# Low parts of the attention output and the gate: from VectorE subtracts to TensorE and ScalarE

## The chip, the cores and the metric

The kernel runs on one core of one Trainium2 chip. The metric is the device time of one execution in microseconds (us), the median of three runs. A NeuronCore has five engines, each with its own in-order queue of instructions: TensorE (PE in the profile; PEld is its weight load), VectorE (DVE), ScalarE (ACT), GpSimd (POOL) and SyncE (SP, which here only issues transfers). They work side by side and wait for one another through semaphores. SBUF is the on-chip memory; PSUM is the memory that TensorE accumulates into, eight banks of 512 float32 columns in 128 partitions.

## The reference

Three stages follow one another; batch 8, sequence 576, eight heads of 64, model width 512, hidden width 2048. The middle one is where the change lies.

```python
# 1: attention inside chunks of 64 tokens
scores = scale * np.matmul(q_c, k_c.transpose(0, 1, 2, 4, 3))
scores = scores - np.max(scores, axis=-1, keepdims=True)
attn = np.exp(scores)
attn = attn / (np.sum(attn, axis=-1, keepdims=True) + 1e-09)
out = np.matmul(attn, v_c)
# 2: x = out with the heads side by side; causal convolution of 5 taps per feature, gate
gate = 1.0 / (1.0 + np.exp(-gate_pre))
val = x @ w_val
y = gate * val @ w_out
# 3: normalised rows, two-layer network, residual
xn = (y - mu) / np.sqrt(var + 1e-06) * g_ln
out = y + np.maximum(xn @ w_ch1, 0.0) @ w_ch2
```

All of it is float32. The large products use a faster float32 form of TensorE that rounds its operands (`fp32r`), and so the kernel splits an operand in a high part (the rounded copy) and a low part (what the rounding took off) and adds three products: high by high, low by high, high by low.

## The kernel before

The 4608 tokens are cut in 18 units of 256 tokens and 9 blocks of 512 (two units each), numbered 0 to 8. A loop of slots, one per unit, carries several stages of different units side by side:

- `a3(u)`: scores of unit u on TensorE (32 small matmuls into `sc`), then the softmax: VectorE takes the maximum (`mx`), subtracts it (`ex`), ScalarE takes the exponential, VectorE sums (`sm`), inverts and multiplies (`pr`).
- `a4(u-1)`: TensorE transposes the probabilities into PSUM (`pst`), ScalarE copies them out (`pT`).
- `a5(u-1)`: TensorE multiplies with v (32 small matmuls into the PSUM tile `x`, features by tokens). ScalarE copies `x` twice: to `xf` (float32, with a halo of four tokens, for the convolution; L233) and to `xh` (the high part; L236). VectorE writes the low part `xl` = `x` - `xh` (L238). Where a sequence ends inside the unit, all of these are cut in two. The tiles `x` and `pst` share one buffer of two PSUM banks.
- `conv(j, f)` for block j and feature tile f (four tiles of 128): one scaled copy on ScalarE (L248) and four steps on VectorE into `cg` (L250), so 16 VectorE steps a block. `sigm(j)`: one sigmoid over the whole of `cg` on ScalarE (L257).
- `val(j, f)`: a chain of 12 matmuls of 512 columns into one PSUM bank (`psv`). VectorE multiplies it with the gate into `gv` in SBUF (L290, in two pieces where a sequence ends inside the block), ScalarE copies `gv` to the high part `gh` (L293), VectorE writes the low part `gl` = `gv` - `gh` (L294).
- `proj(j, t)`: four chains of 12 matmuls (`pso`) from `gh`, `gl` and the output weights; ScalarE copies the result to `y` and sends it to memory.

Between these, VectorE, ScalarE and GpSimd decode and split weights (lines 87 to 96: `da`, and the tiles that are made from it).

The order in which each engine meets its instructions is fixed when the program is built. For the first four slots TensorE's order is as written; after that a list scheduler places all instructions by its own estimate of when they become ready, and pieces under `tc.high_priority()` go first. Within a block of the steady stretch TensorE's order is: value chains 0 and 1, scores, value chain 2, transposes, value chain 3, `x`, projection chains 0 and 1, scores, projection chain 2, transposes, projection chain 3, `x`. After the attention (331 us into the span) comes the two-layer network, which the change does not touch.

Of the kernel before, what the change touches and what calls it, by code (L numbers as in the profile page):

```python
# [8 lines left out]
F32 = mybir.dt.float32  # L9
F32R = mybir.dt.float32r  # L10
U32 = mybir.dt.uint32
ACTF = mybir.ActivationFunctionType
ALU = mybir.AluOpType
# [6 lines left out]
def tile_chunk_attention_gated_mlp(ctx: ExitStack, tc: tile.TileContext, qk, v, w_val, conv_w, w_out, g_ln, w1, w2, out):  # L20
    nc = tc.nc
# [9 lines left out]
    P = 128  # L31
    BLK = 512
    UN = 256
    UPB = BLK // UN
    NB = NT // BLK
    NU = NT // UN
    NP = H // 2
# [3 lines left out]
    LAG = 1  # L41
# [28 lines left out]

    ident = const.tile([P, P], F32, name="ident")
    cw = const.tile([P, (KC + 1) * CT], F32, name="cw")
    gr = const.tile([CT, P], F32, name="gr")


# [112 lines left out]
            nc.scalar.activation(out=t, in_=ps, func=ACTF.Copy)  # L188
            pT[u] = t

    xf, xh, xl = {}, {}, {}

    def new_block(j):
        o = boundary(j)
# [13 lines left out]
    def a5(u):  # L208
# [4 lines left out]
        for i in range(NP // 2):  # L213
            for c in range(NC):
                n, cs = c // 2, slice(c % 2 * CH, (c % 2 + 1) * CH)
                for f in range(2):
                    for r in range(2):
                        r0, o0 = CH * r, CH * f
                        nc.tensor.matmul(
                            out=x[o0:o0 + CH, r, i, c * CH:(c + 1) * CH],  # L220
                            lhsT=va[r0:r0 + CH, c, 2 * i + f, :],
                            rhs=t[r0:r0 + CH, n * NP + 2 * i + f, cs],
                            start=True, stop=True,
                        )
        if uu == 0:
            new_block(j)
# [3 lines left out]
        with tc.high_priority():  # L230
            for lo, hi, sh in segs:
                dst = xf[j][:, :, lo + sh:hi + sh].rearrange("p (r i) t -> p r i t", r=2)
                nc.scalar.activation(out=dst, in_=x[:, :, :, lo - a:hi - a], func=ACTF.Copy)  # L233
            for lo, hi, sh in segs:
                dst = xh[j][:, :, lo:hi].rearrange("p (r i) t -> p r i t", r=2)
                nc.scalar.activation(out=dst, in_=x[:, :, :, lo - a:hi - a], func=ACTF.Copy)  # L236
                low = xl[j][:, :, lo:hi].rearrange("p (r i) t -> p r i t", r=2)
                nc.vector.tensor_tensor(out=low, in0=x[:, :, :, lo - a:hi - a], in1=dst, op=ALU.subtract)  # L238


    cg = pD1.tile([P, CT, BLK + HALO], F32, name="cg")

# [31 lines left out]
    def val(j, f):  # L274
# [8 lines left out]
            ops += [(hs[c][:, fs], xh[j][:, c, :]), (hs[c][:, fs], xl[j][:, c, :]), (ls[c][:, fs], xh[j][:, c, :])]  # L283
        chain(ps, ops)
        o = boundary(j)
        gv = pD2.tile([P, BLK], F32, tag="gv", name="gv")
        with tc.high_priority():
            for lo, hi, sh in ((0, o, 0), (o, BLK, HALO)):
                if lo < hi:
                    nc.vector.tensor_tensor(out=gv[:, lo:hi], in0=ps[:, lo:hi], in1=cg[:, f, lo + sh:hi + sh], op=ALU.mult)  # L290
            a = pD1.tile([P, BLK], F32R, tag=f"gh{f}", name="gh")
            b = pD1.tile([P, BLK], F32R, tag=f"gl{f}", name="gl")
            nc.scalar.activation(out=a, in_=gv, func=ACTF.Copy)  # L293
            nc.vector.tensor_tensor(out=b, in0=gv, in1=a, op=ALU.subtract)  # L294
        gh[j, f], gl[j, f] = a, b

    def proj(j, t):
        hs, ls = wv["os"]
# [285 lines left out]


    make_identity(nc, ident)
    load_qkv(0)
    load_w(w_val, "v", 0)
    load_qkv(1)
# [12 lines left out]
    def slot(u):  # L602
# [14 lines left out]
        if LAG <= u < NU + LAG:  # L617
            a5(u - LAG)
        warm(u, 3)
        for fn in d[2] + d[3]:  # L620
            fn()

    dense = {}
# [1 line left out]
    def at(u, i, fn):  # L625
        dense.setdefault((u, i), []).append(fn)
# [42 lines left out]
    for j in range(NB):  # L669
# [11 lines left out]
            at(u + 1, 2, lambda j=j: sigm(j))  # L681
        for f in range(CT):
            at(*[(u + 1, 2), (u + 1, 3), (u + 2, 0), (u + 2, 1)][f], lambda j=j, f=f: val(j, f))
        for t in range(BLK // P):
            at(*[(u + 2, 2), (u + 2, 3), (u + 3, 0), (u + 3, 1)][t], lambda j=j, t=t: proj(j, t))
    for f in range(NFA):
# [122 lines left out]
```

## Time and profile before

| | |
|---|---|
| median of three runs | 1122.77 us (1122.62 to 1123.02) |
| the profiled execution | 1124.26 us, its span 1122.4 us |
| busy: PE, PEld | 1069.3 us (95%), 866.7 us (77%) |
| busy: DVE, ACT, POOL | 715.7 us (64%), 482.0 us (43%), 108.8 us (10%) |

The span is what the profiler saw of the program; the rest of the execution's time lies around it. A share of busy time is a mean over stages with different limits. TensorE's matmuls are pipelined, so their durations overlap and the distance from one start to the next tells what one costs. In a timeline, "[idle before <-releaser]" is the time for which the engine stood before the instruction, and what ended it.

### The profile page before, as it was taken

Reading aid. Unit: us, or ns where it says so; the run is one execution under the profiler, and the core shown is the slowest. Engines: PE = TensorE matmul, PEld = TensorE weight load, DVE = VectorE, ACT = ScalarE, POOL = GpSimd, SP = SyncE. Lnnn points to the kernel's source line nnn. Section 1 sums busy time; section 2 is a strip of 40 time slices with the busy share of each in tenths; the row PEclk is TensorE's granted clock in tenths of the full one; section 3 lists DMA queues with packets and bytes.
Section 4 is the critical chain, followed back from the end, with each engine's and each line's share of the span. In section 5 each row is a group of like instructions: output and inputs, shape, how many; then the busy total and the mean of one; then the engine's idle time right before and its main releaser. Section 6 shows DMA issues by size and latency. Waiting matters only on the chain.

```text
span 1122.4 us, 17077 instructions
## 1 busy us (share of the span) xinstructions
PE 1069.3 (95%) x6862; PEld 866.7 (77%) x6862; DVE 715.7 (64%) x1171; ACT 482.0 (43%) x832; POOL 108.8 (10%) x120
## 2 busy tenths in 40 slices
PE   5798999999998988899999999999999999999998
PEld 5676777777786866688888788888888888878877
DVE  6999999999949877446557434457443547432434
ACT  3576666766666654344433233333233333121221
POOL 2021100000004434222210000000000000000000
PEclk9898999999999999999999999999999999999999
DMA  8544554551245635343344533233533223622212
GB/s 338 171 142 160 172 177 142 198 181 47 71 165 187 209 112 211 137 150 131 115 149 131 194 107 113 94 113 124 195 113 113 85 94 108 211 94 94 75 38 75
DMA packets 58581, 155.28 MB, mean 138 GB/s; under 512 B 5742, under 2 KB 13958, under 8 KB 56198
## 3 DMA queue, kind: packets, MB, share of 16 engines
q1 hardware_dynamic: 53318, 144.75, 37.8%
q10 hardware_dynamic: 5184, 9.44, 2.3%
q8 instruction: 54, 0.88, 0.3%
q14 instruction: 25, 0.20, 0.1%
HBM read 116.41 MB, written 37.75 MB: 137 GB/s over the span
## 4 chain that ended last, share of the span: by engine, by line
PE 62%; DVE 27%; issue 4%; ACT 4%; DMA 2%; POOL 0%; SPq 0%; POOLq 0%; ACTq 0%; DVEq 0%
PE acc L507 15%; PE x L533 15%; PE psf L507 15%; PE zy L533 10%; DVE cg L250 8%; DVE da L90 2%; DVE da L89 2%; DVE mx L167 2%; DVE sm L176 2%; DVE xl L238 1%; PE acc L393 1%; DVE gv L290 1%; DVE pr L179 1%; DVE gl L294 1%; PE pso L264 1%
## 5 line engine op out<-in xcount | busy, mean ns | idle before, releaser
L553 DVE TENSOR_TENSOR c<-x,c 128x512 f32<-128x512 f32 x96 | 66.2, 690 | 237.6 <-ACT c L549 181.6
L507 PE MATMUL acc<-w,h 128*128 128x512 f32 x768 | 186.8, 392 | 0.0
L507 PE MATMUL psf<-w,h 128*128 128x512 f32 x768 | 186.0, 391 | 0.0
L507 PEld LDWEIGHTS acc<-w,h 128*128 128x128 f32 x768 | 144.9, 189 | 31.7
L507 PEld LDWEIGHTS psf<-w,h 128*128 128x128 f32 x768 | 144.2, 188 | 31.3
L533 PE MATMUL x<-t,wc 128*128 128x512 f32 x576 | 146.9, 390 | 3.4 <-DVE c L553 3.4
L549 ACT ACTIVATE c<-zy 128x512 f32<-128x512 f32 x96 | 57.9, 604 | 188.8 <-PE zy L533 188.7
L533 PEld LDWEIGHTS x<-t,wc 128*128 128x128 f32 x576 | 108.0, 188 | 27.3 <-DVE c L553 4.3
L544 ACT ACTIVATE h<-c 128x512 fp32r<-128x512 f32 x96 | 60.5, 630 | 136.7 <-DVE c L553 136.1
L250 DVE SCALAR_TENSOR_TENSOR cg<-xf,cw,cg 128x516 f32<-128x516 f32 (+1 forms) x176 | 109.1, 660 | 0.1
L512 DVE TENSOR_TENSOR yt<-psf,yt 128x512 f32<-128x512 f32 x128 | 88.1, 690 | 25.1 <-PE psf L507 21.1
L533 PE MATMUL zy<-b,wc 128*128 128x512 f32 x384 | 98.9, 393 | 0.0
L533 PEld LDWEIGHTS zy<-b,wc 128*128 128x128 f32 x384 | 71.2, 188 | 14.6
L545 DVE SCALAR_TENSOR_TENSOR h<-c,h 128x512 fp32r<-128x512 f32 x96 | 68.4, 713 | 14.1 <-ACT h L544 13.9
L264 PE MATMUL pso<-oh,gh 128*128 128x512 f32 x144 | 60.8, 423 | 5.6 <-ACT gh L293 5.4
L264 PE MATMUL pso<-oh,gl 128*128 128x512 f32 x144 | 57.7, 411 | 6.7 <-DVE gl L294 6.7
L96 POOL TENSOR_TENSOR w<-da,w 128x512 fp32r<-128x512 f32 x32 | 47.5, 1489 | 136.6 <-ACT w L95 135.3
L264 PE MATMUL psv<-xh,vh 128*128 128x512 f32 x144 | 59.1, 411 | 0.0
L264 PE MATMUL pso<-ol,gh 128*128 128x512 f32 x144 | 57.9, 402 | 0.0
L264 PE MATMUL psv<-xl,vh 128*128 128x512 f32 x144 | 56.7, 393 | 0.0
L264 PE MATMUL psv<-xh,vl 128*128 128x512 f32 x144 | 56.6, 393 | 0.0
L533 PE MATMUL x<-b,wc 128*128 128x512 f32 x192 | 52.2, 408 | 4.4 <-DVE h L545 3.7
(108 smaller groups left out, 1556.6 us busy)
## 6 DMA issues: line engine op xcount, KB each, us to landing
wc<-wc SPq DMA_DIRECT2D x112, 512.0 KB, 3.3
qkr<-in_qk SPq DMA_DIRECT2D x18, 1024.0 KB, 6.1
raw<-in_moe_w_ch SPq DMA_DIRECT2D x32, 512.0 KB, 4.1
vr<-in_v SPq DMA_DIRECT2D x18, 512.0 KB, 4.4
yd<-y ACTq DMA_DIRECT2D x36, 256.0 KB, 2.6
out<-yt SPq DMA_DIRECT2D x36, 256.0 KB, 3.7
yr<-yd SPq DMA_DIRECT2D x32, 256.0 KB, 3.4
yt<-yd SPq DMA_DIRECT2D x32, 256.0 KB, 4.1
```

What stands on the lines that cost most here:

```text
L89: nc.vector.scalar_tensor_tensor(out=au, in0=hw, scalar=0x80000000, in1=au, op0=ALU.bitwise_and, op1=ALU.bitwise_or)
L90: nc.vector.scalar_tensor_tensor(out=au, in0=lw, scalar=29, in1=au, op0=ALU.logical_shift_right, op1=ALU.bitwise_or)
L96: nc.gpsimd.tensor_tensor(out=lo, in0=a, in1=hi, op=ALU.subtract)
L250: nc.vector.scalar_tensor_tensor(out=o, in0=x[:, f, i + lo:i + hi], scalar=cw[:, i * CT + f:i * CT + f + 1], in1=o, op0=ALU.mult, op1=ALU.add,
L264: nc.tensor.matmul(out=ps, lhsT=lt, rhs=rh, start=(i == 0), stop=(i == n - 1))
L507: nc.tensor.matmul(out=ps, lhsT=lt, rhs=rh, start=(g == 0 and k == 0 and (first or half)), stop=(g == 1 and k == 2 and (last or half)),)
L512: nc.vector.tensor_tensor(out=yt[i], in0=ps, in1=yt[i], op=ALU.add)
L533: nc.tensor.matmul(out=ps, lhsT=lt, rhs=rh, start=(start and c == 0 and i == 0), stop=(c == 1 and i == 2), skip_group_check=True)
L544: nc.scalar.activation(out=t[:, 0, :], in_=src, func=ACTF.Relu)
L545: nc.vector.scalar_tensor_tensor(out=t[:, 1, :], in0=src, scalar=0.0, in1=t[:, 0, :], op0=ALU.max, op1=ALU.subtract)
L549: nc.scalar.activation(out=t, in_=zy, func=ACTF.Copy)
L553: nc.vector.tensor_tensor(out=t, in0=x, in1=t, op=ALU.add)
```

## The change

Both subtracts leave VectorE. A constant `neg`, minus the identity, is made once. For the attention output, the tile `x` stays open in PSUM; once `xh` is copied, two matmuls of 512 columns (a new function `a6`, after the second group of a slot's dense work) add `neg` times `xh` onto it, and ScalarE copies what is left, now the low part, to `xl`. For the gate, VectorE multiplies in place, in the PSUM bank of the value chain; ScalarE copies `gh` from there; a new function `low` adds `neg` times `gh` onto the bank and ScalarE copies the rest to `gl`. The tile `gv` is gone. `xh` and `xl` are no longer cut where a sequence ends. The argument `dynamic_dma_scratch_size=1024` sets the room kept in SBUF for transfers that are described at run time.

```diff
+    neg = const.tile([P, P], F32R, name="neg")
...
-                            start=True, stop=True,
+                            start=(i == 0 and c == 0), stop=False, skip_group_check=True,
...
-            for lo, hi, sh in segs:
-                dst = xh[j][:, :, lo:hi].rearrange("p (r i) t -> p r i t", r=2)
-                nc.scalar.activation(out=dst, in_=x[:, :, :, lo - a:hi - a], func=ACTF.Copy)
-                low = xl[j][:, :, lo:hi].rearrange("p (r i) t -> p r i t", r=2)
-                nc.vector.tensor_tensor(out=low, in0=x[:, :, :, lo - a:hi - a], in1=dst, op=ALU.subtract)
-
+            nc.scalar.activation(out=xh[j][:, :, a:b].rearrange("p (r i) t -> p r i t", r=2), in_=x, func=ACTF.Copy)
+        xq[u] = x
+
+    def a6(u):
+        x = xq.pop(u)
+        j, uu = divmod(u, UPB)
+        a, b = uu * UN, (uu + 1) * UN
+        n = NP // 2
+        for r in range(2):
+            nc.tensor.matmul(
+                out=x[:, r].rearrange("p i t -> p (i t)"), lhsT=neg, rhs=xh[j][:, r * n:(r + 1) * n, a:b],
+                start=False, stop=True, skip_group_check=True,
+            )
+        with tc.high_priority():
+            nc.scalar.activation(out=xl[j][:, :, a:b].rearrange("p (r i) t -> p r i t", r=2), in_=x, func=ACTF.Copy)
...
-                    nc.vector.tensor_tensor(out=gv[:, lo:hi], in0=ps[:, lo:hi], in1=cg[:, f, lo + sh:hi + sh], op=ALU.mult)
-            a = pD1.tile([P, BLK], F32R, tag=f"gh{f}", name="gh")
-            b = pD1.tile([P, BLK], F32R, tag=f"gl{f}", name="gl")
-            nc.scalar.activation(out=a, in_=gv, func=ACTF.Copy)
-            nc.vector.tensor_tensor(out=b, in0=gv, in1=a, op=ALU.subtract)
-        gh[j, f], gl[j, f] = a, b
+                    nc.vector.tensor_tensor(out=ps[:, lo:hi], in0=ps[:, lo:hi], in1=cg[:, f, lo + sh:hi + sh], op=ALU.mult)
+            a = gh[j, f] = pD1.tile([P, BLK], F32R, tag=f"gh{f}", name="gh")
+            nc.scalar.activation(out=a, in_=ps, func=ACTF.Copy)
+        gps[j, f] = ps
+
+    gps = {}
+
+    def low(j, f):
+        ps = gps.pop((j, f))
+        nc.tensor.matmul(out=ps, lhsT=neg, rhs=gh[j, f], start=False, stop=True, skip_group_check=True)
+        with tc.high_priority():
+            b = gl[j, f] = pD1.tile([P, BLK], F32R, tag=f"gl{f}", name="gl")
+            nc.scalar.activation(out=b, in_=ps, func=ACTF.Copy)
...
+            at(*[(u + 1, 3), (u + 2, 0), (u + 2, 1), (u + 2, 1)][f], lambda j=j, f=f: low(j, f))
```

The scheduler's order changes with it. First TensorE, block 6, from the end of the second value chain to the start of the third, before (numbers tell one buffer of a name from another; `vh3_275` is the high part of the value weights' fourth tile; line numbers grow by ten to seventeen in the changed kernel):

```order
L264 MATMUL psv_2882<-xl_2498,vh3_275 128x512
L264 MATMUL psv_2882<-xh_2497,vl3_276 128x512
L162 MATMUL sc_2902<-qkr_2543 64x64 x32
L264 MATMUL psv_2944<-xh_2497,vh0_248 128x512
L264 MATMUL psv_2944<-xl_2498,vh0_248 128x512
L264 MATMUL psv_2944<-xh_2497,vl0_249 128x512
```

And now, where `psv_2881` is the bank of the first value chain of the block and `psv_2904` of the second:

```order
L274 MATMUL psv_2904<-xl_2516,vh3_277 128x512
L274 MATMUL psv_2904<-xh_2515,vl3_278 128x512
L163 MATMUL sc_2921<-qkr_2560 64x64 x22
L308 MATMUL psv_2881<-gh_2896,neg_142 128x512
L163 MATMUL sc_2921<-qkr_2560 64x64 x10
L308 MATMUL psv_2904<-gh_2919,neg_142 128x512
L274 MATMUL psv_2966<-xh_2515,vh0_250 128x512
L274 MATMUL psv_2966<-xl_2516,vh0_250 128x512
```

The first chain's subtracting matmul stands inside the scores, and the second's ahead of the third value chain.

TensorE a little later in block 6, from the end of the last value chain to the start of the projection, before:

```order
L264 MATMUL psv_2975<-xl_2498,vh3_275 128x512
L264 MATMUL psv_2975<-xh_2497,vl3_276 128x512
L219 MATMUL x_2995<-pT_2964,vr_2364 64x64 x32
L264 MATMUL pso_3034<-oh0_559,gh_2878 128x512
L264 MATMUL pso_3034<-ol0_560,gh_2878 128x512
L264 MATMUL pso_3034<-oh0_559,gl_2879 128x512
```

And now:

```order
L274 MATMUL psv_2997<-xl_2516,vh3_277 128x512
L274 MATMUL psv_2997<-xh_2515,vl3_278 128x512
L308 MATMUL psv_2966<-gh_2981,neg_142 128x512
L220 MATMUL x_3017<-pT_2983,vr_2382 64x64 x32
L274 MATMUL pso_3053<-oh0_565,gh_2896 128x512
L274 MATMUL pso_3053<-ol0_566,gh_2896 128x512
L308 MATMUL psv_2997<-gh_3012,neg_142 128x512
L274 MATMUL pso_3053<-oh0_565,gl_2902 128x512
```

The third chain's subtracting matmul stands ahead of `x`, and the last chain's two matmuls into the projection.

ScalarE in block 6, from `xf` and `xh` of the second unit past the sigmoid (the `cg` row) to the next exponential, before:

```order
L233 ACTIVATE xf_2853<-x_2820 128x4x256
L236 ACTIVATE xh_2856<-x_2820 128x4x256
L257 ACT_TABLE_LOAD
L257 ACTIVATE cg_147<-cg_147 128x2064
L293 ACTIVATE gh_2878<-gv_2875 128x512
L293 ACTIVATE gh_2898<-gv_2895 128x512
L188 ACTIVATE pT_2964<-pst_2965 128x1024
L293 ACTIVATE gh_2960<-gv_2957 128x512
L174 ACT_TABLE_LOAD
L174 ACTIVATE ex0_143<-ex0_143 128x16x64
L293 ACTIVATE gh_2991<-gv_2988 128x512
```

And now:

```order
L234 ACTIVATE xf_2873<-x_2840 128x4x256
L235 ACTIVATE xh_2876<-x_2840 128x4x256
L267 ACT_TABLE_LOAD
L267 ACTIVATE cg_148<-cg_148 128x2064
L249 ACTIVATE xl_2877<-x_2840 128x4x256
L301 ACTIVATE gh_2896<-psv_2881 128x512
L301 ACTIVATE gh_2919<-psv_2904 128x512
L311 ACTIVATE gl_2902<-psv_2881 128x512
L311 ACTIVATE gl_2964<-psv_2904 128x512
L175 ACT_TABLE_LOAD
L175 ACTIVATE ex0_144<-ex0_144 128x16x64
```

The copy to `xl` stands between the sigmoid and the first `gh`, and two copies to `gl` ahead of the exponential.

## Rows read from the trace of the kernel before

**Rows 1.** windows of the six blocks: us, busy (instructions) by engine, clock, DMA share, GB/s
```profile
87.83:123.52 35.69, 32.63 (x374) 25.21 (x369) 35.08 (x51) 22.71 (x30) 4.23 (x4) 0.90 0.46 156
123.52:155.61 32.09, 30.35 (x375) 23.68 (x369) 31.66 (x47) 21.88 (x29) 3.29 (x4) 1.00 0.51 173
155.61:189.10 33.49, 31.27 (x375) 24.75 (x369) 33.45 (x49) 21.29 (x27) 3.09 (x4) 0.95 0.50 166
189.10:219.94 30.84, 29.50 (x375) 23.31 (x369) 30.72 (x48) 21.00 (x28) 1.86 (x3) 1.00 0.51 180
219.94:251.05 31.11, 29.47 (x374) 23.31 (x368) 30.42 (x47) 19.21 (x25) 0.57 (x2) 1.00 0.51 179
251.05:281.37 30.32, 29.42 (x376) 23.32 (x369) 27.62 (x42) 19.25 (x25) 0.32 (x1) 1.00 0.15 54
```

**Rows 2.** timeline of TensorE around a run of `x`: start, us, instruction, [idle before]
```profile
218.53 0.39 PE L264 MATMUL pso<-oh,gl 128*128 128x512 f32 x1
218.85 1.16 PE L219 MATMUL x<-pT,vr 64*64 64x64 f32 x64
219.94 0.50 PE L264 MATMUL psv<-xh,vh 128*128 128x512 f32 x1
```

**Rows 3.** timeline of TensorE, block 6, from the projection's first matmul
```profile
265.47 0.50 PE L264 MATMUL pso<-oh,gh 128*128 128x512 f32 x1
...
267.20 0.39 PE L264 MATMUL pso<-ol,gh 128*128 128x512 f32 x1
267.42 0.39 PE L264 MATMUL pso<-oh,gl 128*128 128x512 f32 x1
268.10 0.50 PE L264 MATMUL pso<-oh,gh 128*128 128x512 f32 x1 [0.29 <-ACT gh L293]
268.43 0.40 PE L264 MATMUL pso<-ol,gh 128*128 128x512 f32 x1
269.44 0.50 PE L264 MATMUL pso<-oh,gl 128*128 128x512 f32 x1 [0.61 <-DVE gl L294]
```

**Rows 4.** groups by line on VectorE, 0 to 336 us: busy, mean ns | idle before
```profile
L294 DVE TENSOR_TENSOR gl<-gv,gh 128x512 fp32r<-128x512 f32 x36 | 26.3, 766 | 0.7 <-ACT gh L293 0.6
...
L238 DVE TENSOR_TENSOR xl<-x,xh 128x1024 fp32r<-128x1024 f32 (+3 forms) x24 | 22.8, 948 | 1.6 <-ACT xh L236 1.6
```

**Rows 5.** timeline of TensorE, scores between projections
```profile
143.26 0.34 PE L162 MATMUL sc<-qkr 64*64 64x64 f32 x6
143.53 0.50 PE L264 MATMUL pso<-oh,gh 128*128 128x512 f32 x1
```

**Rows 6.** timeline of ScalarE, block 6
```profile
252.12 1.02 ACT L236 ACTIVATE xh<-x 128x1024 fp32r<-128x1024 f32 x1
...
258.12 1.93 ACT L257 ACTIVATE cg<-cg 128x2064 f32<-128x2064 f32 x1 [3.68 <-DVE cg L250]
...
267.43 0.61 ACT L293 ACTIVATE gh<-gv 128x512 fp32r<-128x512 f32 x1
```

**Rows 7.** timeline of VectorE, block 6
```profile
260.08 1.42 DVE L290 TENSOR_TENSOR gv<-psv,cg 128x384 f32<-128x384 f32 x4 [2.00 <-ACT cg L257]
...
271.60 2.08 DVE L250 SCALAR_TENSOR_TENSOR cg<-xf,cw,cg 128x516 f32<-128x516 f32 x3
...
276.59 1.22 DVE L167 TENSOR_REDUCE mx<-sc 128x16 f32<-128x1024 f32 x1
```

**Rows 8.** timeline of VectorE, the first unit
```profile
31.09 0.69 DVE L89 SCALAR_TENSOR_TENSOR da<-raw,da 128x512 uint32<-128x512 uint32 x1
...
34.12 1.22 DVE L238 TENSOR_TENSOR xl<-x,xh 128x1024 fp32r<-128x1024 f32 x1 [1.61 <-ACT xh L236]
35.26 0.87 DVE L250 SCALAR_TENSOR_TENSOR cg<-xf,cw,cg 128x256 f32<-128x256 f32 x2
```

**Rows 9.** TensorE's timeline at its longest idle time, and the window around it
```profile
173.31 0.50 PE L264 MATMUL pso<-oh,gl 128*128 128x512 f32 x1 [2.22 <-DVE gl L294]
...
170.00:178.40 8.40, 6.18 (x52) 4.41 (x44) 8.37 (x13) 6.75 (x11) 1.69 (x2) 0.80 0.49 159
```

More of the change, by code (lines that the diff above doesn't have):

```diff
@@ L189, in a4 @@
             pT[u] = t
-    xf, xh, xl = {}, {}, {}
+    xf, xh, xl, xq = {}, {}, {}, {}
     def new_block(j):
@@ L285, in val @@
         o = boundary(j)
-        gv = pD2.tile([P, BLK], F32, tag="gv", name="gv")
         with tc.high_priority():
@@ L586, in tile_chunk_attention_gated_mlp @@
     make_identity(nc, ident)
+    nc.vector.tensor_scalar(out=neg, in0=ident, scalar1=-1.0, scalar2=None, op0=ALU.mult)
     load_qkv(0)
@@ L619, in slot @@
         warm(u, 3)
-        for fn in d[2] + d[3]:
+        for fn in d[2]:
+            fn()
+        if LAG <= u < NU + LAG:
+            a6(u - LAG)
+        for fn in d[3]:
             fn()
@@ L788, in turned @@
         return chunks(a).transpose(0, 2, 5, 3, 1, 4).reshape(18, 128, 1, 4, 256)
-    nc = bacc.Bacc("TRN2", target_bir_lowering=False, num_devices=1)
+    nc = bacc.Bacc("TRN2", target_bir_lowering=False, num_devices=1, dynamic_dma_scratch_size=1024)
     data = {
```

## The prediction

> **What bounds the kernel now.** I read four views in this order. First the windows cut at the starts of the value chains: one window per block of 512 tokens [rows 1]. The reader should see that VectorE is busy for 35.08 of 35.69, 31.66 of 32.09 and 33.45 of 33.49 us in blocks 1 to 3, so it looks like the bound; but in block 6 it is busy for 27.62 of 30.32 us only, and the block is the shortest. Then TensorE's timeline. A run of 64 small matmuls (64x64, here `x`) takes 1.09 us from its first start to the next large one, with no wait on either side [rows 2]; a 512-column matmul starts 0.23 us after the one before it (267.20 to 267.42 [rows 3], and so in every gapless chain). In block 6 TensorE waits in one place only, at the turn from the value chains to the projection: 268.10 - 267.42 - 0.23 = 0.45 us for `gh` and 269.44 - 268.43 - 0.23 = 0.78 us for `gl` of the last feature tile [rows 3], and each restart costs 0.11 more (0.33 to 0.34 instead of 0.23 to the next start). So TensorE's own work in a block is 30.32 - 1.23 - 0.22 = 28.9 us, and even the best block has only 1.4 us that VectorE could give back. Blocks 4, 5 and 6 (30.84, 31.11, 30.32) are within 1.4 to 2.2 us of TensorE's own time; blocks 1 to 3 have 6.8, 3.2 and 4.6 us of waiting. After 331 us the program is not touched and TensorE sets its pace; it only moves with the end of the projection.
>
> **What is removed.** 24 `xl` subtracts (22.8 us) and 36 `gl` subtracts (26.3 us) leave VectorE [rows 4], 49 us in all, about 5 us of each block. What VectorE gives up shortens the program only where TensorE waits for it, so this is worth at most the waits listed above: 14.6 us in blocks 1 to 3, 5.6 us in blocks 4 to 6.
>
> **What is added, TensorE.** 18 units with two matmuls and 9 blocks with four: 72 matmuls of 512 columns. By the step of [rows 3] they cost 72 x 0.23 = 16.4 us, and TensorE has nothing to hide them behind: 8 x 0.23 = 1.8 us in every block. The order shows that the first of a block's four cuts the 32 score matmuls in two. What a cut costs is seen where a run of six stands between projections: it takes 0.27 us where 6 of 64 would be 0.10 [rows 5], and a large matmul behind a break takes 0.33 to the next start instead of 0.23 (268.10 to 268.43 [rows 3]); with the entry to the second piece I take 0.4 us. So a block without any wait becomes 28.9 + 1.8 + 0.4 = 31.1 us: more than block 6 takes today.
>
> The Trainium skill's page "TensorE: Matmul & The Clock Gate", section "Back-to-back issue gap", gives about 131 ns for each pair of weight load and 512-column matmul in a sustained stream. By it the 72 would cost 9.4 us (an estimate from that page). The trace does not agree: 0.23 us from start to start in a gapless chain [rows 3]; the measurement decides, and nothing above uses the page.
>
> **What is added, ScalarE.** The low parts are now 18 copies of 1024 elements and 36 of 512. By `xh` (1.02 us) and `gh` (0.61) [rows 6] that is 18 x 1.02 + 36 x 0.61 = 40 us, 4.5 us a block on an engine that is busy for 19 to 22 us of 31 [rows 1]. As a sum it fits. As a queue it matters, below.
>
> **The new wait.** Today nothing on TensorE needs the gate before the projection begins. In the new order the subtracting matmul of the first feature tile stands inside the score matmuls, some 7 us into the block, and the score run's rest, two value chains, the transposes and the projection queue behind it. It needs `gh`, which needs the gate product, which needs the sigmoid of the whole block, which needs the last of 16 convolution steps. I add that chain from T, the end of the `x` run ahead of the projection.
> - ScalarE: first part of `xf`, last `gl`, `xh`, first `cg`: about 0.25 + 1.0 + 0.55 + 0.95 + 0.65 (the last like a `gh`); the convolution can start at T + 3.4 (now 271.60 - 265.47 = T + 6.1 [rows 3, 7], as VectorE is late).
> - VectorE: 16 steps at 0.67 (three end to end take 2.08, the last of them 0.75) and four softmax steps at 1.14 to 1.22 with a reciprocal: 10.7 + 4.8 = 15.5 [rows 7]. Last step at T + 18.9.
> - Sigmoid 1.93 [rows 6]: T + 20.9. Behind it on ScalarE the `xl` copy (0.95) now stands ahead of `gh`; the gate product (four pieces 1.42 [rows 7], the first tile's done after 1.1) is hidden by it. `gh` 0.61, and some 0.05 for each of the four hops: T + 22.7.
> - TensorE gets there after four projection chains, scores, transposes, `x`, two value chains, five added matmuls and two thirds of the scores: T + 21.8.
>
> So TensorE stands for about 1.0 us at this place (with the restart) in each block without weight decoding, and the block takes 32.1 us. The turn to the projection in [rows 3] no longer waits: the last `gh` and `gl` don't queue behind VectorE's softmax any more.
>
> **Sum.**
> - Blocks 3 to 6: 4 x 32.1 = 128.4 against 33.49 + 30.84 + 31.11 + 30.32 = 125.8 [rows 1]: +2.6. Bounds: -1.4 without the wait, +6 if it is twice as long.
> - Blocks 1 and 2: VectorE also decodes the first expert weights here; in the new order six decoding steps (two of about 0.35 and four of 0.6 as the one at 31.09 [rows 8]: 3.1 us) stand between the last convolution step and the gate product. The wait becomes about 2.4 and 2.1 us, with 0.6 to 1.3 more at the second and fourth subtracting matmul: 34.7 + 33.6 = 68.3 against 67.8 [rows 1]: +0.5. Bounds: 2 x 31.1 = 62.2 gives -5.6; +4 if the clock falls (below).
> - Up to 88 us: without `xl` the first convolution starts 0.8 us sooner (`xl` ends where it begins [rows 8]). But the new order does all of unit 3's convolution steps ahead of its softmax sum, and puts that unit's transposes before the third value chain instead of after it, so TensorE waits for `pr` there, then for the first `gh`; by adding durations block 1 starts 0.5 us later. Bounds: -4 (four `xl`, four `gl` come off and TensorE uses half) to +3.
> - Blocks 7 and 8: ten added matmuls and a cut, 2.7, less one wait as in [rows 3], 1.4, and eight more copies on a full ScalarE, 0.7: +2. Bounds 0 to +3.
> - The gate product written into PSUM: no row shows VectorE writing there. From the rows it lies between nothing and the 0.07 us by which a dependent step (0.67) exceeds an independent one (0.60) [rows 4, 7]; I take nothing. Doubled, it would add 0.6 us to the chain above in each block.
>
> Together +5.6 on the span of 1122.4, so 1128.0. The profiled execution took 1124.26 us, 1.9 around its span and 0.13% above the median 1122.77; added to the median the forecast is 1128.4, and I say 1128.
>
> **Rivals.**
> 1. VectorE is the bound and the waits go. For it: blocks 1 to 3 in [rows 1]. Then blocks 1 to 6 take 6 x 31.1 = 186.6 instead of 193.5, the start gains 3, the end loses 1: -9, 1114 us. It decides if the sigmoid ends more than 1 us earlier than I add up, so that the subtracting matmul never waits. Against it: block 6, where VectorE has slack and the sum still comes out longer. The Trainium skill's "Perfetto Trace Analysis", section "Optimizing Scalar/DVE Operations", stands on this rival's side: with VectorE saturated, moving work to ScalarE may make sense. The trace agrees on the saturation in blocks 1 to 3 and not in block 6. Chance 0.21.
> 2. Gains of 2 to 3 us in the early blocks cancel the losses of the late ones: 1121 to 1125. Chance 0.21.
> 3. The waits of over 2 us in blocks 1 and 2 take the clock down. In the trace TensorE sat idle for 2.22 us at 173.31, and the granted clock of the 8.4 us around it is 0.80 [rows 9]: 3.4 us of them at half (1.2 instead of 2.4 GHz), so 1.7 us of work lost on top of the wait. Two such places, or one and the doubled gate product: 1132 to 1137. Chance 0.13.
>
> That the subtracts are still done on VectorE can be excluded: the order has none.
>
> **Numbers.** My own case (1126 to 1132) 0.45, the rivals as above. This kernel's measurements can tell about 0.2% (2.2 us) from no change. Faster 0.21, same 0.21, slower 0.58. The range from 1116 to 1135 leaves out the best part of rival 1 and the worst of rival 3.
>
> **What would show it.** In the new profile: TensorE idle ahead of the first subtracting matmul of each block, released by ScalarE's `gh`, 1 us in late blocks and over 2 in blocks 1 and 2; no wait at the projection's first chain; VectorE some 25 us busy of 32 in blocks 3 to 6; blocks 3 to 6 at 32 us. I am wrong if these blocks take 31 us or less, if block 1 starts before 85 us, or if that idle time is absent.

## The result and the profile after

The changed kernel takes 1135.13 us (median of four runs, 1132.82 to 1138.91) against 1122.69: 1.0117 times as long, 95% interval 1.0083 to 1.0151. It is slower, as forecast, but by 12.4 us in the medians where I had 5.6, and just above my range. The profiled execution took 1132.82 us, its span 1131.0.

The windows of blocks 0 to 6, cut at the value chains' starts as in [rows 1] (same columns; the first is block 0):

```profile
54.90:92.32 37.42, 33.78 (x381) 26.86 (x377) 32.67 (x47) 27.91 (x39) 7.37 (x7) 0.93 0.49 162
92.32:130.63 38.31, 34.10 (x383) 26.57 (x377) 34.53 (x54) 30.10 (x42) 8.50 (x7) 0.96 0.57 193
130.63:163.94 33.31, 31.99 (x383) 25.25 (x377) 27.48 (x43) 24.08 (x31) 0.31 (x2) 1.00 0.56 191
163.94:195.94 32.00, 31.25 (x382) 25.14 (x376) 24.17 (x35) 23.57 (x29) 0.31 (x2) 1.00 0.40 133
195.94:227.90 31.96, 31.25 (x383) 25.14 (x376) 24.06 (x35) 23.61 (x30) 0.31 (x2) 1.00 0.39 133
227.90:259.92 32.02, 31.23 (x382) 25.15 (x376) 23.91 (x35) 23.62 (x30) 0.31 (x2) 1.00 0.41 133
259.92:292.02 32.10, 31.24 (x382) 25.15 (x376) 23.82 (x35) 23.61 (x30) 0.20 (x1) 1.00 0.15 51
```

Blocks 3 to 6 take 32.0 us each; VectorE is busy for 24 of them. Block 0 of the kernel before, which [rows 1] do not have:

```profile
55.59:87.83 32.24, 31.19 (x373) 24.39 (x369) 32.21 (x47) 22.64 (x32) 6.38 (x6) 0.97 0.45 148
```

Block 1 starts at 92.32 us instead of 87.83 and block 3 at 163.94 instead of 155.61: that is 8.3 us, of which I had forecast 1.0. The network starts at 344.70 instead of 330.88.

TensorE's timeline in block 6 (start, us, instruction, idle time before it): the subtracting matmul in the scores, where the prediction put it.

```profile
266.07 0.91 PE L163 MATMUL sc<-qkr 64*64 64x64 f32 x44
267.84 0.49 PE L308 MATMUL psv<-gh,neg 128*128 128x512 f32 x1 [0.86 <-ACT gh L301]
268.26 0.56 PE L163 MATMUL sc<-qkr 64*64 64x64 f32 x20
268.76 0.50 PE L308 MATMUL psv<-gh,neg 128*128 128x512 f32 x1
```

The same place in block 1, and the window over what follows:

```profile
99.60 0.91 PE L163 MATMUL sc<-qkr 64*64 64x64 f32 x44
103.11 0.50 PE L308 MATMUL psv<-gh,neg 128*128 128x512 f32 x1 [2.60 <-ACT gh L301]
...
104.97 0.63 PE L274 MATMUL psv<-xl,vh 128*128 128x512 f32 x1
105.39 0.63 PE L274 MATMUL psv<-xh,vl 128*128 128x512 f32 x1
...
103.00:107.00 4.00, 3.89 (x28) 3.00 (x29) 2.37 (x4) 2.71 (x6) 1.55 (x2) 0.65 0.95 349
```

After 2.60 us of idle time matmuls start 0.42 us apart instead of 0.23; the granted clock of the 4 us is 0.65, a mix of 2.4 GHz and 1.2. Block 0 waits for `gh` twice:

```profile
66.43 0.65 PE L308 MATMUL psv<-gh,neg 128*128 128x512 f32 x1 [2.46 <-ACT gh L301]
...
76.49 0.49 PE L308 MATMUL psv<-gh,neg 128*128 128x512 f32 x1 [1.18 <-ACT gh L301]
```

VectorE's groups: decoding (L91 is the last of a tile's three steps) from the start of block 0 to block 3, and the gate product up to the network.

```profile
L91 DVE SCALAR_TENSOR_TENSOR da<-raw,da 128x512 uint32<-128x512 uint32 x13 | 8.7, 684 | 0.1
...
L299 DVE TENSOR_TENSOR psv<-psv,cg 128x64 f32<-128x64 f32 (+7 forms) x64 | 28.3, 462 | 28.7 <-PE psv L274 14.6 <-ACT cg L267 13.3
```

The same two of the kernel before, the decoding first from block 0 to block 3, then from there to block 7:

```profile
L90 DVE SCALAR_TENSOR_TENSOR da<-raw,da 128x512 uint32<-128x512 uint32 x8 | 5.5, 683 | 0.1
...
L90 DVE SCALAR_TENSOR_TENSOR da<-raw,da 128x512 uint32<-128x512 uint32 x6 | 5.1, 849 | 0.0
...
L290 DVE TENSOR_TENSOR gv<-psv,cg 128x384 f32<-128x384 f32 (+7 forms) x64 | 25.0, 446 | 7.6 <-ACT cg L257 7.6
```

Thirteen weight tiles are now decoded in blocks 0 to 2 and none in 3 to 6; before, seven and six (the line counts eight, but the first of them began at 55.11, ahead of block 0). In the new order the network's first weights come forward into the room that the subtracts left. What that does in block 1 is seen on VectorE, from the first convolution steps to the gate product:

```profile
80.67 8.54 DVE L260 SCALAR_TENSOR_TENSOR cg<-xf,cw,cg 128x516 f32<-128x516 f32 x9 [0.56 <-ACT cg L258]
...
98.45 0.76 DVE L89 TENSOR_SCALAR da<-da 128x512 uint32<-128x512 uint32 x2
99.12 1.29 DVE L90 SCALAR_TENSOR_TENSOR da<-raw,da 128x512 uint32<-128x512 uint32 x2
100.33 1.29 DVE L91 SCALAR_TENSOR_TENSOR da<-raw,da 128x512 uint32<-128x512 uint32 x2
101.53 1.69 DVE L299 TENSOR_TENSOR psv<-psv,cg 128x64 f32<-128x64 f32 x4
```

Two tiles (3.1 us) stand ahead of the gate product, and nine convolution steps take 8.54 us, not 9 x 0.67 = 6.0: two of them met GpSimd's subtracts for decoded tiles.

### The profile page after: what moved, and what is told of

Same layout as the page of the kernel before. It is cut to its first block, busy times and chain, and to the rows that moved or that the text cites. A ratio compares the mean times of both kernels' runs of the same rounds, so it can differ in the third digit from the quotient of the medians.

```text
span 1131.0 us, 17186 instructions
## 1 busy us (share of the span) xinstructions
PE 1085.9 (96%) x6934; PEld 882.6 (78%) x6934; DVE 677.7 (60%) x1112; ACT 518.8 (46%) x880; POOL 109.5 (10%) x120
## 4 chain that ended last, share of the span: by engine, by line
PE 69%; DVE 19%; ACT 7%; issue 3%; DMA 1%; POOL 1%; SPq 0%; ACTq 0%; DVEq 0%; POOLq 0%
PE acc L523 16%; PE x L549 15%; PE psf L523 14%; PE zy L549 10%; DVE cg L260 6%; PE psv L274 5%; PE pso L274 2%; DVE da L90 2%; DVE da L91 1%; PE acc L409 1%; DVE h L561 1%; ACT cg L267 1%; PE pst L372 1%; DVE psv L299 1%; PE psh L274 1%
## 5 line engine op out<-in xcount | busy, mean ns | idle before, releaser
L549 PE MATMUL x<-t,wc 128*128 128x512 f32 x576 | 149.2, 395 | 3.5 <-DVE c L569 3.5
L274 PE MATMUL pso<-oh,gh 128*128 128x512 f32 x144 | 58.4, 406 | 0.0
L560 ACT ACTIVATE h<-x 128x512 fp32r<-128x512 f32 x32 | 19.2, 600 | 82.3 <-PE x L549 82.3
L417 POOL TENSOR_TENSOR wc<-raws,wc 128x256 fp32r<-128x256 f32 x56 | 46.3, 850 | 104.3 <-ACT wc L416 99.2
```

What stands on the lines that cost most here:

```text
L274: nc.tensor.matmul(out=ps, lhsT=lt, rhs=rh, start=(i == 0), stop=(i == n - 1))
L417: eng.tensor_tensor(out=lo, in0=a, in1=hi, op=ALU.subtract)
L549: nc.tensor.matmul(out=ps, lhsT=lt, rhs=rh, start=(start and c == 0 and i == 0), stop=(c == 1 and i == 2), skip_group_check=True)
L560: nc.scalar.activation(out=t[:, 0, :], in_=src, func=ACTF.Relu)
```

## The experiments

My theory after the result: TensorE pays in full for the 72 matmuls, waits at those that need `gh`, and VectorE's relief brings nothing because ScalarE and the decoding take it up. Rivals: the waits are the main loss; or ScalarE's queue; or the later stages moved by themselves. All ratios are to the kernel before in runs on the same chip, with their 95% intervals.

**A ladder between the two kernels.** First the subtracts taken away with nothing in their place.

```diff
-                nc.vector.tensor_tensor(out=low, in0=x[:, :, :, lo - a:hi - a], in1=dst, op=ALU.subtract)
...
-            nc.vector.tensor_tensor(out=b, in0=gv, in1=a, op=ALU.subtract)
-        gh[j, f], gl[j, f] = a, b
+        gh[j, f] = gl[j, f] = a
```

> The kernel before without the 24 xl and 36 gl subtracts and with nothing in their place (the chains read the high part where they read the low part, so the low parts are left out of the result; TensorE's count is the same). It measures what VectorE's relief is worth at most. Theory 1 (the copies on ScalarE, in front of gh and pT in its queue, are what ate the relief in the kernel without subtracting matmuls, 1119.8): late blocks 28.9 us, blocks 1 to 3 together 90 to 94 instead of 101.3, total 1102 to 1108. Theory 2 (VectorE was never what TensorE waited for beyond 2 or 3 us): 1116 to 1120, as that kernel.

1108.5 us, 0.9893 (0.9871 to 0.9915): theory 1, at its upper edge, with the late blocks as expected and blocks 1 to 3 at 96.1 us, not the 90 to 94 that I had. Then with the gate product in PSUM:

```diff
-                    nc.vector.tensor_tensor(out=gv[:, lo:hi], in0=ps[:, lo:hi], in1=cg[:, f, lo + sh:hi + sh], op=ALU.mult)
+                    nc.vector.tensor_tensor(out=ps[:, lo:hi], in0=ps[:, lo:hi], in1=cg[:, f, lo + sh:hi + sh], op=ALU.mult)
```

> The kernel before without the xl and gl subtracts (1108.5; the low parts are left out there too), and the gate product written in place in PSUM as in the changed kernel, gh copied from there. Against that run it adds nothing but the in-place product; against the kernel without subtracting matmuls (1119.8) it lacks ScalarE's 54 copies. If the copies in ScalarE's queue are what ate VectorE's relief: late blocks 28.8 to 28.9 us, total 1106 to 1111. If the product in PSUM is (slower, or its bank held too long): late blocks 29.5 us or more, total 1114 to 1120.

1112.8 us, 0.9915 (0.9891 to 0.9939): between the two. Next the changed kernel without its subtracting matmuls:

```diff
-        nc.tensor.matmul(out=ps, lhsT=neg, rhs=gh[j, f], start=False, stop=True, skip_group_check=True)
```

(and the two in `a6`).

> The changed kernel without its 72 subtracting matmuls (ScalarE's copies read PSUM as it stands, so the low parts hold the whole value; all other work is there). VectorE and ScalarE have the work of the changed kernel, TensorE that of the kernel before, and nothing on TensorE needs the gate before the projection. My theory (the loss is the added matmuls and the waits in their queue): late blocks at 29 to 29.5 us instead of 32.0, block 1 starts by 86 us, total 1105 to 1112. Rival A (ScalarE's extra copies in its queue are what costs): late blocks stay over 31 us, total over 1122. Rival B (the later stages moved by themselves, the blocks are only where it shows): total near 1130.

1119.8 us, 0.9979 (0.9970 to 0.9989): my expectation was 8 us too low, and rival A's time was not reached either. Then with the matmuls, but free of waits:

```diff
+        ops.append((neg[:, 0:P], neg))
         chain(ps, ops)
```

(`neg` holds zeros and is 512 columns wide; two such matmuls follow each run of `x`).

> The 72 added matmuls stay, but with zeros as operands and as the last of their own chains, so that they need neither the gate nor the high parts (the subtraction is left out, as in the kernel without the matmuls). Against that kernel it adds matmul work alone; against the changed kernel it takes away the waits and the cut of the scores. My theory: 72 x 0.23 = 16.4 us above the kernel without matmuls, late blocks 30.7 to 31.0 us, total 1121 to 1128, so 8 to 12 us below the changed kernel, most of it before 130 us. Rival C (matmul work is the whole loss, the waits are only slack that shows at another place): the same as the changed kernel, 1132 to 1138.

1138.0 us, 1.0139 (1.0122 to 1.0156): no faster than the changed kernel, so rival C. Blocks from 3 on of each (columns as above), first without the subtracts:

```profile
240.72:269.56 28.84, 28.84 (x374) 23.47 (x369) 23.32 (x35) 19.50 (x25) 0.20 (x1) 1.00 0.16 56
```

with the product in PSUM:

```profile
241.71:271.30 29.59, 28.91 (x375) 23.47 (x369) 23.62 (x35) 19.02 (x25) 0.20 (x1) 1.00 0.16 55
```

with ScalarE's copies too:

```profile
157.03:191.59 34.56, 31.51 (x375) 25.57 (x369) 29.82 (x46) 24.51 (x32) 0.31 (x2) 0.90 0.53 183
191.59:220.43 28.84, 28.84 (x375) 23.47 (x369) 22.44 (x33) 21.97 (x29) 0.31 (x2) 1.00 0.43 147
220.43:251.08 30.65, 28.90 (x374) 23.46 (x369) 23.38 (x35) 22.83 (x31) 0.31 (x2) 1.00 0.44 139
```

and with 72 matmuls that wait for nothing:

```profile
166.63:197.35 30.72, 30.72 (x378) 24.96 (x376) 23.77 (x36) 22.36 (x29) 0.31 (x2) 1.00 0.46 162
...
228.95:261.21 32.26, 30.79 (x377) 24.96 (x376) 23.76 (x35) 22.89 (x31) 0.31 (x2) 1.00 0.40 132
```

28.84 us without any idle time is the 28.9 of the prediction, TensorE's own work, and 30.72 the same with eight added matmuls. The third run's blocks are uneven: block 3, with three decoded tiles, takes 34.56, block 4 28.84, block 5 30.65, block 6 29.79. What comes on top in block 5 is seen on TensorE at the end of the value chains:

```profile
234.12 0.39 PE L269 MATMUL pso<-oh,gl 128*128 128x512 f32 x1
236.25 0.93 PE L220 MATMUL x<-pT,vr 64*64 64x64 f32 x48 [1.75 <-ACT pT L189]
```

and on ScalarE in the same run:

```profile
230.85 0.60 ACT L296 ACTIVATE gh<-psv 128x512 fp32r<-128x512 f32 x1 [1.29 <-DVE psv L294]
231.35 0.59 ACT L305 ACTIVATE gl<-psv 128x512 fp32r<-128x512 f32 x1
231.82 0.61 ACT L296 ACTIVATE gh<-psv 128x512 fp32r<-128x512 f32 x1
232.30 0.62 ACT L305 ACTIVATE gl<-psv 128x512 fp32r<-128x512 f32 x1
232.94 1.28 ACT L175 ACT_TABLE_LOAD   x1
234.23 1.06 ACT L175 ACTIVATE ex<-ex 128x1024 f32<-128x1024 f32 x1
235.19 1.00 ACT L189 ACTIVATE pT<-pst 128x1024 f32<-128x1024 f32 x1
```

The two `gl` copies stand ahead of the exponential and of `pT`, for which the next `x` waits. So the steps are, of 1122 us: VectorE's relief -12.0, the product in PSUM +2.5, ScalarE's copies +7.2, the matmuls as work and the waits for `pT` +18.0, their real places -2.5. By the intervals each step is uncertain by 2 to 4 us, so the two of 2.5 us are not told from nothing by the time alone. (At the network's start: 317.5, 319.2, 330.8, 347.0, 344.7 us; the matmuls' step there is 16.2.) The step called ScalarE's copies hardly stands in the late blocks: blocks 4 to 6 together take 88.9 us without the copies and 89.3 with them. Blocks 0 to 3, which decode twelve tiles in both runs, take 125.6 and 134.0. The copies' run also holds `x` until `xl` is read, copies `xh` whole and has the argument `dynamic_dma_scratch_size`. Some 3 of these 8.3 us are a lower granted clock (0.90 in block 3, which also has 3.05 us of idle time); that ScalarE's queue is behind the rest is argued and not shown. What in the in-place product costs 0.75 us in a late block I did not find: the multiplication itself hardly (462 ns against 446); TensorE waits for `pT` there too.

**Each half alone.** The attention part with the gate's low part as before,

```diff
+            nc.vector.tensor_tensor(out=b, in0=gv, in1=a, op=ALU.subtract)
...
-            at(*[(u + 1, 3), (u + 2, 0), (u + 2, 1), (u + 2, 1)][f], lambda j=j, f=f: low(j, f))
```

and the gate's part with `xl` as before:

```diff
+                nc.vector.tensor_tensor(out=low_, in0=x[:, :, :, lo - a:hi - a], in1=dst, op=ALU.subtract)
...
-            a6(u - LAG)
```

> Only the attention output's low part goes by TensorE and ScalarE; the gate's low part is VectorE's subtract from SBUF as before. 36 added matmuls, no wait for the gate in TensorE's queue. My theory: late blocks 30.9 us (28.9 + 4 x 0.23 + the turn's waits of 1.2), early blocks gain from VectorE's relief; total 1119 to 1126, block 1 starts by 88 us. Rival C (matmul work alone, half of it): half of the loss, 1129. Rival A (ScalarE): late blocks over 31.5.

> Only the gate's low part goes by TensorE and ScalarE; xl is VectorE's subtract as before. The scheduler puts the first subtracting matmul behind the scores here, in block 0 behind the next scores. My theory: 36 added matmuls cost 8.3 us, the waits are smaller than in the changed kernel except in block 0; late blocks 31 to 32 us, total 1124 to 1132. Rival C: half of the loss, 1129; if the wait for the gate is nearly all of the loss wherever the matmul stands: 1132 or more.

Attention part: 1113.8 us, 0.9919 (0.9899 to 0.9939), below the theory's range. Gate part: 1131.3 us, 1.0079 (1.0059 to 1.0099), within it, its late blocks 31.7 to 32.5 us. The attention part's blocks 4 to 6 have no idle time at all:

```profile
217.03:246.83 29.80, 29.80 (x378) 24.22 (x372) 25.83 (x39) 21.16 (x26) 0.81 (x2) 1.00 0.42 142
```

29.80 = 28.84 + 4 x 0.23 + 0.04: the matmuls at their price, and all waits of [rows 3] gone. Relieving VectorE of `xl` alone is enough for that, so in a late block the gate's part has nothing left to win and adds its own matmuls, the in-place product and the queue. In block 0 the gate's part is the loss too: 37.50 us with it alone, 31.54 with the attention part alone.

**The place of the wait.**

```diff
-            at(*[(u + 1, 3), (u + 2, 0), (u + 2, 1), (u + 2, 1)][f], lambda j=j, f=f: low(j, f))
+            at(*[(u + 2, 1), (u + 2, 1), (u + 2, 1), (u + 2, 1)][f], lambda j=j, f=f: low(j, f))
```

> The changed kernel with all four gate subtracting matmuls of a block behind the third value chain and the transposes, so none stands inside the scores. Same work on every engine. If the wait at the first subtracting matmul and the cut of the scores are what my prediction says they are: late blocks 30.7 us instead of 32.0 (28.9 + 8 x 0.23), early blocks lose 2 to 4 us of their waits and the half clock behind them; total 1120 to 1126. If matmul work alone is the loss, or the wait only moves to the projection's first gl: late blocks stay at 31.5 to 32, total 1130 to 1136.

1133.2 us, 1.0115 (1.0092 to 1.0139): in the second range, though not by its reason. Late blocks take 31.35 us without idle time, so the wait and the cut of the scores are worth 0.65 us in each; the cuts of `x` and of the projection keep the rest. Block 0 takes 33.86 us instead of 37.42 and block 1 starts at 88.60, 3.7 us earlier, but blocks 1 and 2 take 40.39 and 35.60 us: by block 3 it is where the changed kernel is (164.59 against 163.94). So the place of that matmul decides block 0, and not blocks 0 to 2 taken together. Here a subtracting matmul cuts a run of `x`:

```profile
241.55 0.56 PE L220 MATMUL x<-pT,vr 64*64 64x64 f32 x18
242.04 0.51 PE L308 MATMUL psv<-gh,neg 128*128 128x512 f32 x1
242.48 0.92 PE L220 MATMUL x<-pT,vr 64*64 64x64 f32 x46
243.33 0.50 PE L274 MATMUL pso<-oh,gh 128*128 128x512 f32 x1
```

**The decoding.** Held back:

```diff
+    def paced_ff(f, j):
+        for _ in range(2 if f == 0 else 1):
+            t = stg.tile([P, DM, 2], U32, tag="raw", name="hold")
+            nc.gpsimd.tensor_copy(out=t[:, 0, 0:1].bitcast(F32), in_=xf[j][:, 0, HALO:HALO + 1])
+        early_ff(f)
```

(one call for each of blocks 3 to 6).

> The changed kernel, with the decoding of the first eight expert weight tiles held back (their staging buffers are first written from xf of blocks 3 to 6, two tiles for each), so that it comes at two tiles a block from block 3 on. In the changed kernel VectorE, freed of the subtracts, decodes five tiles in block 1 and three in block 2 (the kernel before: two and two). If this decoding, put in front of the gate product and gh, is why blocks 1 and 2 take 71.6 us and not the 68.3 that I forecast: block 1 at 32 to 33.5 us, block 2 at 32, blocks 3 to 6 at 32.5 to 33.5 (they have the decoding now), total 1126 to 1130. If the waits of the early blocks come from elsewhere (the loads, the clock, ScalarE's copies by themselves): block 1 stays over 36 us and the total over 1132.

> The control: the kernel before with the same holding back. Its decoding is spread over blocks 1 to 5 at two tiles a block already, so holding it back to blocks 3 to 6 only moves 3.6 us a block from blocks 1 and 2 to later ones: blocks 1 and 2 at 32 and 30.5, blocks 3 to 6 at 31 to 33.5, total 1117 to 1124, within 0.4% of the kernel before. If holding back by itself gains as much as in the other two (6 us or more), the decoding is no part of what the change did.

> The attention part alone with the same holding back of the decoding. Blocks 1 and 2 (35.4 and 32.8 us, VectorE busy for all of it) lose eight decoded tiles of 1.8 us: 29.8 to 31 us each; blocks 3 to 6 take them into VectorE's slack of 4 to 5 us and stay at 29.8 to 30.5. Total 1104 to 1108, below every other version. Rival: the waits of blocks 1 and 2 only move to blocks 3 to 6, total 1112 to 1116.

Changed kernel: 1131.7 us, 1.0077 (1.0060 to 1.0094), block 1 and block 5:

```profile
89.85:121.25 31.40, 31.23 (x382) 25.15 (x377) 23.41 (x34) 23.62 (x30) 0.31 (x2) 1.00 0.39 135
...
222.16:255.70 33.54, 32.46 (x382) 25.34 (x376) 28.32 (x43) 27.45 (x37) 3.82 (x5) 1.00 0.66 221
```

Block 1 without decoding takes 31.40 instead of 38.31 us, but block 0, with two tiles instead of five, still 36.87 instead of 37.42. Block 3 starts 9.0 us earlier (154.98) with nine tiles fewer decoded: 1.0 us a tile. But blocks 3 to 6 take 33.4 to 34.7, and at block 7 (290.42 against 292.02) nearly all is given back. So the decoding says where the early loss stands, not how large the whole is; my 1126 to 1130 was too low. The control took 1118.3 us, 0.9962 (0.9948 to 0.9977), block 1 in 30.48. Holding back gains 0.4% in both kernels, and the changed one stays 1.0115 times the other (1.0077 / 0.9962), as without (1.0117): where the decoding stands explains nothing of the total. With the decoding placed nearly alike in both, the network starts at 343.43 and 327.11 us, 16.3 us apart; this difference holds waits and VectorE's relief beside the matmuls. The attention part with it: 1114.4 us, 0.9936 (0.9913 to 0.9959), the same as without: its rival was right, blocks 1 and 2 at 29.80 and 32.32 but 3 to 6 at 31.5 to 33.7.

Then by which engine a tile costs. ScalarE's first step on GpSimd:

```diff
-        nc.scalar.activation(out=a, in_=hw.bitcast(F32), func=ACTF.Copy, scale=2.0 ** -112)
+            nc.gpsimd.tensor_scalar(out=a, in0=hw.bitcast(F32), scalar1=2.0 ** -112, scalar2=None, op0=ALU.mult)
```

> The changed kernel; the first step of decoding the eight early expert weight tiles (a scaled copy of 0.6 us, which waits for the tile's load, up to 2.2 us in one place) goes to GpSimd instead of ScalarE, in whose queue gh, pT and the sigmoid stand behind it. Order on VectorE and the number of tiles in each block stay. If ScalarE's stall for a load in front of gh makes the early blocks long: blocks 1 and 2 at 68 to 69.5 us instead of 71.6, total 3 to 5 us below the changed kernel (1130 to 1132). If it is VectorE's decoding itself (1.8 us a tile ahead of the gate product): 71 to 73 us, total 1133 to 1137.

> The attention part alone (1113.8) with the same. In that run ScalarE waited 6.1 us in five places for the loads in blocks 1 and 2, and TensorE 4.1 us for pT. If that is the cause: blocks 1 and 2 at 63 to 66 us instead of 68.2, total 1109 to 1112; else 1112 to 1117.

1140.9 us, 1.0163 (1.0134 to 1.0192), and 1126.8 us, 1.0031 (1.0018 to 1.0045). The edit also caught tiles decoded after the network's start (8 and 6 us more up to its first `zy`), so only the blocks count: block 3 starts at 163.38 and 156.27 us, as without the edit (163.94, 156.33). So nothing is won; since GpSimd's copy can itself hold VectorE up (see the last section), this doesn't exclude ScalarE's stall for loads. A third run, with the decoding held back too, gave 1127.6 us, 1.0056 (1.0031 to 1.0081), and the same answer: blocks 3 to 6 at 32.3 to 34.3 us.

GpSimd's subtract for the eight tiles left out (`if eng is not None`), or put on VectorE (`eng = nc.vector`):

> The changed kernel without GpSimd's subtracts for the eight early expert weight tiles (their low parts are left out, the high part is read twice); VectorE's and ScalarE's decoding stays. In the changed kernel two convolution steps of block 1 that met such a subtract took 1.8 us instead of 0.75, and ended 0.55 us after it. If it is this by which a decoded tile makes blocks 0 to 2 long: the start to block 3 (163.9 us there) falls to 157 to 160, total 1128 to 1131. If VectorE's own steps (1.8 us a tile) are what costs: block 3 starts at 162 to 165, total 1132 to 1137.

> The changed kernel with these eight subtracts on VectorE (0.7 us each) instead of GpSimd (1.3 to 1.7). By the first theory a tile costs 0.7 us of VectorE instead of about 1.0 of standing still: block 3 starts 1 to 3 us earlier than in the changed kernel, total 1130 to 1134. By the second it costs 0.7 more: block 3 starts 3 to 5 us later, total 1135 to 1140, unless the scheduler moves the decoding.

> The attention part alone with the eight subtracts on VectorE. In this order the scheduler spreads the decoding over blocks 1 to 5, two tiles a block, as in the kernel before. If GpSimd's work beside VectorE's is what a decoded tile costs: blocks 1 to 5 at 30 to 32 us, total 1108 to 1112, below the attention part as it is (1113.8); else 1113 to 1118.

1131.3 us, 1.0077 (1.0062 to 1.0092), block 3 at 162.28; 1131.6 us, 1.0083 (1.0058 to 1.0108), block 3 at 161.63; 1113.7 us, 0.9920 (0.9905 to 0.9935). Left out, GpSimd's subtracts gave back 1.7 us of the nine, which speaks for VectorE's own three steps (1.8 us a tile); but with 0.7 us more of VectorE's work in their place, and again thirteen tiles in blocks 0 to 2, block 3 came 2.3 us earlier, which speaks for the first theory, and the attention part gained nothing, which doesn't. How the 1.0 us of a tile divides stays open.

**A better version.** The attention part alone beats both kernels; with the subtracts on VectorE it is the same within the intervals. Its blocks 1 and 2 still take 35.39 and 32.82 us, with VectorE busy for 35.16 and 32.41. The gate's low part on GpSimd, in three blocks or in all:

```diff
-            nc.vector.tensor_tensor(out=b, in0=gv, in1=a, op=ALU.subtract)
+            (nc.gpsimd if j < 3 else nc.vector).tensor_tensor(out=b, in0=gv, in1=a, op=ALU.subtract)
```

> Attention part alone as in the run of 1113.8, and the gate's low part by a subtract on GpSimd instead of VectorE in blocks 0 to 2, where VectorE was busy for 35.2 of 35.4 and 32.4 of 32.8 us. If VectorE is the bound there: about 2.9 us less VectorE work a block, block 1 at 32.5 to 33.5, block 2 at 30.5 to 31.5, total 1108 to 1111. Rival (GpSimd and VectorE slow each other down, as VectorE's decoding step that took 1.41 us instead of 0.69 while GpSimd worked): blocks 1 and 2 as long as with VectorE or longer, total 1113 to 1117.

> As the last, but GpSimd's subtract in all blocks. From block 3 on VectorE has slack and TensorE doesn't wait (29.80 us a block in the attention-only run), so nothing is to be won there; if GpSimd takes over 1 us for a subtract, the projection's first chain waits for the last gl: 0.5 to 1 us a block, total 2 to 5 us above the last kernel. Rival (it is hidden): the same as the last kernel.

1116.9 us, 0.9969 (0.9948 to 0.9990), and 1121.5 us, 0.9998 (0.9984 to 1.0012): the rival for the first, and the second 4.6 us above it, as expected. In the first, blocks 1 and 2 take 34.14 and 34.16 us, together as long as with VectorE's subtracts, and block 0 36.57 instead of 31.54: there the loss stands. GpSimd in block 1 of the first,

```profile
108.39 1.28 POOL L304 TENSOR_TENSOR gl<-gv,gh 128x512 fp32r<-128x512 f32 x1 [4.08 <-ACT gh L303]
...
111.07 1.53 POOL L304 TENSOR_TENSOR gl<-gv,gh 128x512 fp32r<-128x512 f32 x1 [0.15 <-ACT gh L303]
```

and VectorE beside it:

```profile
108.44 1.23 DVE L177 TENSOR_REDUCE sm<-ex 128x16 f32<-128x1040 f32 x1
...
111.39 2.29 DVE L180 TENSOR_TENSOR pr<-ex,sm 128x1024 f32<-128x1024 f32 x1
```

`pr` takes 2.29 us instead of 1.22. From block 3 on the blocks are 29.80 in both; in the last two blocks the second loses 3.7 us against the first, not in every block as I expected.

## Why the prediction was right in sign and wrong in size

- TensorE's work: right. 28.9 us of its own in a block was measured as 28.84. In blocks without idle time four added matmuls cost 0.96 us (29.80) and eight 1.88 (30.72), so 0.23 to 0.24 each and 16.9 to 17.3 for all 72, where I had 16.4. By the Trainium skill's "TensorE: Matmul & The Clock Gate", section "Back-to-back issue gap", it would have been 9.4; the runs don't agree.
- The new wait, late blocks: right. 0.71 to 0.86 us of idle time at the place named, blocks at 32.0 us (forecast 32.1), blocks 3 to 6 together 128.1 (128.4); VectorE 24 us busy. The turn to the projection waits no more.
- Up to 88 us: this term failed most. Forecast +0.5, measured +4.5, above my bound of +3. I had TensorE wait for `pr`, then for the first `gh`, and let VectorE's relief pay for most of it. In block 0 there is no wait for `pr` and two for `gh`, 2.46 and 1.18 us. The block is 5.2 us longer than before: TensorE is idle for 3.6 us instead of 1.1, and the granted clock of 0.93 instead of 0.97 costs 2.6 us of work instead of 1.0. The decoding is not why: with it held back the block takes 36.87, and with the attention part alone, at four tiles, 31.54. With those of the gate further back it takes 33.86. So the gate's subtracting matmuls, waiting for `gh`, make block 0 long. Without any such wait nothing is won all the same: in that run block 0 takes 31.05, but it starts 5.5 us later, behind a wait of 6.69 us for `pr`.
- Blocks 1 and 2: this term failed in block 1. Forecast 68.3, measured 71.6: block 2 took 33.31 where I had 33.6, block 1 38.31 where I had 34.7. The wait of 2.4 us was right in block 1 (2.60) and too long in block 2 (1.08). What I had not in the sum: in block 1 the half clock of rival 3 stands behind the wait, my bound "+4 if the clock falls" (0.96 granted over 38.31 us, 1.5 us of work), and TensorE waits 0.84 us for `xh` at 96.17. Some 1.5 us I can't place for certain; the two subtracting matmuls that cut a run of `x` there are part of it. The waits come with the decoding: without it the block takes 31.40. I counted the decoding between the last convolution step and the gate product, and not the tiles that the new order had moved into the rest of these blocks (before block 3 it is 11 of the network's tiles instead of 5), nor their meeting with GpSimd.
- What was removed: right as a size and wrong as a credit. The relief is worth 12.0 us by itself; I had bounded it by the waits, 14.6 and 5.6. Of those 14.6 TensorE's idle time in [rows 1] is only 7.0 (35.69 - 32.63, 32.09 - 30.35, 33.49 - 31.27); 5.2 of the rest is the granted clock of 0.90 and 0.95. I let the relief pay for the matmuls in the early blocks. By the ladder, the step of ScalarE's copies takes 7.2 of it, and the in-place product, costed at nothing, 0.75 us in a late block. For ScalarE's queue I followed `gh` alone; `pT` stands in it too, and the order shown ahead of the prediction has `gl` ahead of the exponential.
- The wait as a loss of its own: overrated. Without it the kernel is no faster (1138.0), since TensorE then waits for `pT`.
- Blocks 7 and 8: +3.2 where I had +2 and a bound of +3. After that the network took 786.3 us instead of 791.5; it took 786 to 792 in all the profiled executions that leave its decoding alone, so I put no mechanism to it. The medians differ by 12.4 us, the network's starts by 13.8; that the profiled spans differ by 8.6 only, nearer to my 5.6, is chance.
- Rival 1 is excluded: VectorE is relieved and the kernel is slower. The Trainium skill's "Perfetto Trace Analysis", section "Optimizing Scalar/DVE Operations", says that with VectorE saturated, moving work to ScalarE may make sense; of the two halves here, which go to TensorE and ScalarE, one gained (0.9919) and one lost (1.0079). Rival 2 is excluded too. Rival 3's time, 1132 to 1137, holds the result, and its mechanism is in the trace, but it does not make the difference: in blocks 0 to 3 the granted clock costs the changed kernel 4.1 us of work and the kernel before 6.2 (0.97, 0.90, 1.00, 0.95).

## What to carry to other kernels

Price an offload by the engine that receives it, instruction by instruction in its queue: what stands behind each new copy, and who waits for that. When a list scheduler places the work, count again what it brings forward into the room that a change makes, in every block and not only on the path looked at: here it moved the loss into the first blocks and left its size. Of two like edits try each alone: here the first takes all the gain (0.9919) and the second only adds work.

## What the runs showed of the hardware

- VectorE steps with two SBUF operands stand still beside a GpSimd subtract that began first: in block 1 of the changed kernel a convolution step takes 0.75 us alone and 1.80 or 1.76 when it meets one, and ends 0.55 us after it; `pr` 2.29 instead of 1.22. A reduction beside one was not slowed (1.23 us). The Trainium skill's "SBUF — State Buffer", section "SBUF: two separate sides", says that GpSimd and a VectorE step with two SBUF inputs shut each other out of a port pair for a whole instruction; these rows agree.
- A scaled copy of 512 columns takes 1.70 us on GpSimd (mean of ten) and 0.65 to 0.70 on ScalarE.
- Cutting a run of 64 small matmuls by one of 512 columns costs TensorE 0.45 us beside the 0.23 of the matmul: in the run with late subtracting matmuls `x` takes 1.78 us from its first start to the next large matmul (241.55 to 243.33), without idle time, where an uncut run takes 1.09 [rows 2].
